# Summing softmax denominators four tiles at a time on VectorE, with a new planning figure for the exponential

## Chip, cores, metric

The kernel runs on one core of one Trainium2 chip. The metric is the device time of one execution in microseconds (us), and the time of a version is the median of its runs.

## What is computed

A pre-normalised transformer layer in bf16 on 2,048 tokens of width 1,024, with 32 heads of 32 columns and a hidden width of 3,584:

```python
h  = x + attention(layernorm(x), wqkv, wo)      # softmax(q k^T / sqrt(32)) v, 32 heads
h2 = h + gelu(layernorm(h) @ w1 + b1) @ w2 + b2
```

Every score is exponentiated once: 2,048 x 2,048 x 32 numbers. Besides the product with V, each row of exponentials must be summed, since that sum is the softmax's denominator.

## The kernel before

**Tiles.** Heads are handled in eight groups of four (g) and queries in eight blocks of 256 (qb), so there are 64 jobs. A job runs eight rounds; a round covers 256 keys. The score product of a round, `qk`, is eight row-tiled matmuls (line 805) into four PSUM banks. ScalarE exponentiates them with two instructions of 128 x 1024 (line 816) into one of nine buffers `PT` (a few early rounds use other buffers, which the profile calls `PX`). The product with V, `pv`, is eight column-tiled matmuls (line 842) which accumulate in one half of a PSUM bank.

**Denominators.** VectorE first adds the two key tiles of a round (line 857, 128 x 1024 bf16 into a ring of three buffers `PS`). TensorE then adds that pair sum over the partitions with four column-tiled matmuls against a tile of ones (`den`, line 871), accumulating in the other half of the job's bank. Round 7 of a job (and every odd round of the first three jobs, the lead) skips VectorE and gives its exponentials to eight `den` matmuls directly. A job so makes seven pair sums, and its `den` of one round is put behind the `pv` of the next. The pair sum has the highest priority on VectorE (-2); draining a projection or an FFN bank has 0, the pieces of the gelu have 1.

**Background.** Everything else on TensorE (projections, output product `wo`, `ffn1`, `ffn2`) is "background". It fills the time between score products. It uses PSUM banks 6 and 7, of which the running job holds one. In the attention the kernel goes through query blocks in order; `wo(u)`, the second layer norm, `ffn1(u)`, the gelu (five VectorE instructions of 128 x 1024 and one tanh on ScalarE per four tiles, lines 1020 to 1025) and `ffn2(u)` of block u run beneath the attention of later blocks. After the last exponential there remain `wo(7)`, layer norm, `ffn1(7)`, half of `ffn2(6)` and `ffn2(7)`.

**What sets the order.** A list scheduler in the kernel's Python simulates all engines with a cost per instruction and writes out one fixed instruction order per engine, with semaphore waits. `c_act` is the planned duration of a ScalarE instruction: for 1,024 columns 0.064 + 1024/1200 = 0.917 us. `c_dve(1024, 2)` plans 0.598 us for a pair sum; a `pv` is planned at 0.22 us, a `den` of one pair sum at 0.11, a change of TensorE's tiling at 0.104. A ready `qk` always goes first on TensorE; background goes in between until the next `qk` is ready in the plan; ready `pv` and `den` wait in a group. Where no background is ready in two stretches of the plan (`KEEP`), dummy matmuls of line 1203 fill in.

The order holds on the chip whatever the real durations are: an engine that gets to an instruction early waits for its semaphore, and one that is late holds up what stands behind it.

Of the kernel before, what the change touches and what calls it, by code (L numbers as in the profile page):

```python
# [8 lines left out]
ALU = mybir.AluOpType  # L9
# [328 lines left out]
def build_kernel(nc, A_x, A_wqkv, A_wo, B_w1, B_b1, B_w2, B_b2, out):  # L338
# [22 lines left out]
    class Area:  # L361
# [3 lines left out]
        def take(self, shape, dtype, align=64):  # L365
            n = mybir.dt.size(dtype)
            for d_ in shape[1:]:
                n *= d_
            self.cur = -(-self.cur // align) * align
            off = self.cur  # L370
            self.cur += n
            assert self.cur <= TOP, (shape, self.cur - TOP)
            return off, n

    def sb(area, name, shape, dtype, split=1, parts=1):


        off, n = area.take(shape, dtype)
        h = nc.alloc_sbuf_tensor_at(name, shape, dtype, offset=off)
        step = n // split  # L380
        bufs = []
        for i in range(split):
            ps = [gr.buf("SB", off + i * step, off + (i + 1) * step, (name, i)) for _ in range(parts)]
            bufs.append(ps if parts > 1 else ps[0])
        return h, (bufs if split > 1 else bufs[0])
# [31 lines left out]
    PS, B_PS = sb(top, "PS", [P, NS, 4, 256], BF, NS)  # L417
# [107 lines left out]
    def c_dve(n, x=1):  # L525
        return (62 + n / x) / 960.0

    def c_act(n, ap_bias=False):
        return (0.064 if n == 1024 else 0.073) + (0.093 if ap_bias else 0.0) + n / 1200.0

    def pe(fns, occ, reads=(), writes=(), kind="bg", mode="full", prio=0, after=()):
        return gr.add(E.PE, fns, occ, 0.225 if isinstance(fns, list) and len(fns) > 1 else 0.2, reads, writes, prio, kind, mode, after)
# [7 lines left out]
    def bi(bank):  # L540
        return bank.n if isinstance(bank, Slot) else bank
# [33 lines left out]
    def act(fn, n, reads=(), writes=(), prio=0, ap_bias=False, kind="", after=()):  # L575
        return gr.add(E.Activation, fn, c_act(n, ap_bias), 0.16, reads, writes, prio, kind, after=after)

    def dve(fn, occ, reads=(), writes=(), prio=0, after=()):
        return gr.add(E.DVE, fn, occ, 0.135, reads, writes, prio, after=after)
# [13 lines left out]
    def dma_transpose(out_ap, in_ap, nbytes, reads, writes, prio):  # L593
# [5 lines left out]
         reads=[B_ident], writes=[B_ident])  # L599
# [222 lines left out]
    PV_START = 6  # L822

    closing = set()

    class Job:

# [7 lines left out]
        def pv(self, r, s):  # L835
            g, bank, first = self.g, self.bank, self.n == 0
            last = self.n == 7
            self.n += 1
            fns = []
            for i in range(2):  # L840
                for h in range(4):
                    fns.append(lambda p, i=i, h=h: p.matmul(  # L842
                        psum[32 * h:32 * h + 32, bi(bank), 0:256], V[:, g, 2 * r + i, 32 * h:32 * h + 32],
                        PTs[s][:, h // 2, h % 2, 256 * i:256 * i + 256], start=first and i == 0, stop=last and i == 1,
                        tile_position=(0, 32 * h), skip_group_check=True))
            rd = B_PTs[s] + [B_V[NT * g + 2 * r], B_V[NT * g + 2 * r + 1]]
            t = pe(fns, 0.22, reads=rd, writes=[self.B_O, self.B_D] if first else [self.B_O], kind="pv", mode="col")
            take(t, bank)
            while self.sums:
                self.den(*self.sums.pop(0), False)  # L850
            if r == 7 or self.g == 0 and self.qb < NLJ and r % 2:
                self.sums.append((s, True))
            else:
                n = cnt["ps"] % NS
                cnt["ps"] += 1
                pairs = PTs[s][:, :, :, :].rearrange("p u j c -> p (u j) c")
                dve(lambda v: v.tensor_tensor(PS[:, n, :, :], pairs[:, :, 0:256], pairs[:, :, 256:512], ALU.add), c_dve(1024, 2),  # L857
                    reads=B_PTs[s], writes=[B_PS[n]], prio=-2, after=hold if self.g == 0 and self.qb < NLJ else ())
                self.sums.append((n, False))
            if last:  # L860
                while self.sums:
                    self.den(*self.sums.pop(0), not self.sums)
                self.finish()
# [199 lines left out]
    for k in range(80):  # L1063
        pe(lambda p: p.matmul(psum[:, 6, 0:256], ident[:, :], b2t[:, 0:256], start=True, stop=True), 0.18 if k < 42 else 0.115,
           reads=[B_ident, B_b2t], writes=[B_ps[6]], kind="warm")
    LEAD_ACT = (0, 1, 2, 3)
    LEAD_PE = 10
    NLJ = 3
# [21 lines left out]
    for hc in range(8):  # L1090
# [7 lines left out]
        for k, r in [(k, hc) for k in range(min(hc, NLJ))] + ([(hc, r) for r in range(hc + 1)] if hc < NLJ else []):  # L1098
            n = 8 * k + r
# [199 lines left out]
def bass_sequential_preLN__softmax_full_mha__dense_activation_gelu__prompt_kernel(  # L1299
    nc: bass.Bass,  # L1300
    A_x: bass.AP,
    A_wqkv: bass.AP,
    A_wo: bass.AP,
    B_x: bass.AP,
    B_w1: bass.AP,
    B_b1: bass.AP,
    B_w2: bass.AP,
    B_b2: bass.AP,
    out: bass.AP,
):  # L1310
    build_kernel(nc, A_x, A_wqkv, A_wo, B_w1, B_b1, B_w2, B_b2, out)
# [28 lines left out]
```

## Time and profile before

| what | before |
|---|---|
| median of 3 runs | 1080.26 us (1077.96 to 1081.25) |
| the profiled execution | 1079.06 us; span in the profile 1077.3 us |
| TensorE busy (modelled ends) | 1053.3 us, 98% |
| ScalarE busy | 1013.3 us, 94% |
| VectorE busy | 747.3 us, 69% |
| granted TensorE clock | 1.0 |
| exponentials | 1,024 of 128 x 1024, from 15.0 us to 1010.8 us |
| pair sums on VectorE (line 857) | 439, 686 ns median duration |

Times in the profile are microseconds from the start of the span. The recorded duration of an instruction includes a part that overlaps its neighbour on the same engine, so durations of a full engine add up to more than its busy time; how often an engine can take such an instruction has to be read from successive starts or successive ends. The chain of waits is followed from the last instruction back to what released it.

### The profile page before, as it was taken

What the parts mean: (1) busy time and instruction counts of PE and PEld (TensorE: products, weight loads), DVE (VectorE), ACT (ScalarE), POOL (GpSimd) and SP (SyncE); (2) the same over time, 40 slices, a digit from 0 to 9 for tenths busy, and PEclk for the clock granted to TensorE, in tenths of its full rate; (3) what the DMA queues carried; (4) which work ended last, traced back from release to release, by engine and by line L of the source; (5) the groups of instructions that cost most, each with busy time, mean ns of one, the idle gap of its engine ahead of it and who ended that gap; (6) DMA issues with size and microseconds to landing.
All of it is one profiled execution on the core that took longest, in us unless ns stands there. A gap on an engine that the chain in (4) does not pass through costs nothing.

```text
span 1077.3 us, 41835 instructions
## 1 busy us (share of the span) xinstructions
PE 1053.3 (98%) x19071; PEld 609.4 (57%) x19071; DVE 747.3 (69%) x1438; ACT 1013.3 (94%) x1116; POOL 45.4 (4%) x110
## 2 busy tenths in 40 slices
PE   8999999999999999999999999999999999999998
PEld 6576555554444754674475457447545754575483
DVE  8776666566576895698489659948975976696401
ACT  4999999999999999999999999999999999999650
POOL 4200000000010000001000100100010000000100
PEclk9999999999999999999999999999999999999999
DMA  8561543438473555655664764466375555866260
GB/s 223 166 172 30 159 134 119 138 119 297 165 186 130 188 191 181 232 181 169 217 240 164 209 230 179 154 223 230 144 232 205 186 200 181 294 220 250 94 244 19
DMA packets 136177, 196.37 MB, mean 182 GB/s; under 512 B 49216, under 2 KB 100288, under 8 KB 133184
## 3 DMA queue, kind: packets, MB, share of 16 engines
q1 hardware_dynamic: 136000, 193.70, 54.0%
q8 instruction: 149, 2.44, 0.9%
q14 instruction: 28, 0.23, 0.1%
HBM read 177.94 MB, written 27.26 MB: 190 GB/s over the span
## 4 chain that ended last, share of the span: by engine, by line
ACT 60%; PE 33%; DVE 4%; POOL 1%; issue 1%; DMA 0%; SPq 0%; POOLq 0%; DVEq 0%
ACT PT L816 55%; PE ps L568 11%; PE ps L565 7%; PE ps L571 5%; PE ps L805 5%; PE ps L842 3%; ACT PX L816 3%; ACT uu L1023 2%; PE ps L871 2%; DVE PS L857 1%; DVE st L617 1%; DMA xrb<-in_A_x_dram 0%; DVE gT L1001 0%; DVE gT L1025 0%; POOL denb L626 0%
## 5 line engine op out<-in xcount | busy, mean ns | idle before, releaser
L816 ACT ACTIVATE PT<-ps 128x1024 bf16<-128x1024 f32 x992 | 922.0, 1094 | 5.9 <-PE ps L805 5.7
L857 DVE TENSOR_TENSOR PS<-PT 128x1024 bf16<-128x1024 bf16 x431 | 285.3, 685 | 132.4 <-PE ps L871 67.6
L805 PE MATMUL ps<-QT,KT 32*128 32x256 bf16 x4096 | 203.9, 273 | 5.6 <-ACT PT L816 2.7
L842 PE MATMUL ps<-PT,V 128*32 128x256 bf16 x3968 | 174.2, 273 | 2.1 <-ACT PT L816 1.7
L805 PEld LDWEIGHTS ps<-QT,KT 32*128 32x128 bf16 x4096 | 61.0, 92 | 161.4 <-ACT PT L816 135.9
L871 PE MATMUL ps<-PS,ones 128*32 128x256 bf16 x1756 | 122.0, 274 | 2.3 <-DVE PS L857 1.2
L842 PEld LDWEIGHTS ps<-PT,V 128*32 128x32 bf16 x3968 | 101.7, 97 | 28.5 <-issue 7.0
L568 PE MATMUL ps<-hnT,a_w1r 128*128 128x256 bf16 x940 | 114.5, 273 | 0.6 <-DVE gT L1001 0.5
L565 PE MATMUL ps<-a_w2r,gT 128*32 128x512 bf16 x1436 | 102.2, 381 | 0.1
L568 PEld LDWEIGHTS ps<-hnT,a_w1r 128*128 128x128 bf16 x940 | 86.8, 98 | 24.4 <-issue 13.7
L568 PE MATMUL ps<-a_w2r,gT 128*128 128x512 bf16 x397 | 97.6, 381 | 0.8 <-DVE hch L966 0.6
L565 PE MATMUL ps<-hnT,a_w1r 128*32 128x256 bf16 x2512 | 89.8, 274 | 3.5 <-DVE OD L894 1.5
L1001 DVE TENSOR_TENSOR gT<-ps,b1f 128x512 bf16<-128x512 f32 x98 | 67.3, 686 | 16.0 <-PE ps L568 8.0
L565 PEld LDWEIGHTS ps<-hnT,a_w1r 128*32 128x32 bf16 x2512 | 61.8, 96 | 19.5 <-issue 16.5
L1046 DVE SCALAR_TENSOR_TENSOR hch<-ps,hch 128x512 bf16<-128x512 f32 x32 | 21.9, 685 | 70.5 <-PE ps L571 47.1
L871 PEld LDWEIGHTS ps<-PS,ones 128*32 128x32 bf16 x1756 | 46.2, 96 | 26.6 <-DVE PS L857 8.6
L568 PEld LDWEIGHTS ps<-a_w2r,gT 128*128 128x128 bf16 x397 | 33.7, 98 | 46.5 <-issue 13.0
L568 PE MATMUL ps<-xnT,Wall 128*128 128x512 bf16 (+1 forms) x272 | 57.4, 346 | 0.4 <-ACT xnT L645 0.2
L1023 ACT ACTIVATE uu<-uu 128x1024 bf16<-128x1024 bf16 x49 | 54.3, 1113 | 0.0
L565 PEld LDWEIGHTS ps<-a_w2r,gT 128*32 128x32 bf16 x1436 | 32.0, 96 | 25.4 <-issue 13.5
L622 POOL CAST mvb<-mv 128x2 bf16<-128x2 f32 (+1 forms) x25 | 5.2, 216 | 972.5 <-DVE mv L619 972.5
L568 PE MATMUL ps<-wov,OT 128*128 128x512 bf16 x146 | 35.4, 380 | 1.4 <-DVE OD L894 0.8
(93 smaller groups left out, 1020.8 us busy)
## 6 DMA issues: line engine op xcount, KB each, us to landing
a_w2r<-w_blocks SPq DMA_DIRECT2D x105, 512.0 KB, 5.2
a_w1r<-w_blocks SPq DMA_DIRECT2D x98, 512.0 KB, 3.5
wov<-wo_blocks SPq DMA_DIRECT2D x16, 1024.0 KB, 4.8
w_blocks<-in_B_w_dram SPq DMA_DIRECT2D x28, 512.0 KB, 3.9
b_w1r<-w_blocks SPq DMA_DIRECT2D x14, 512.0 KB, 3.9
a_w1r<-in_A_wqkv_dram SPq DMA_DIRECT2D x11, 512.0 KB, 5.5
Wall<-in_A_wqkv_dram SPq DMA_DIRECT2D x17, 256.0 KB, 4.9
xrb<-in_A_x_dram SPq DMA_DIRECT2D x16, 256.0 KB, 4.7
```

Of the source, the lines that this page charges most:

```text
L565: fns.append(lambda p, j=j: p.matmul(psum[32 * j:32 * j + 32, bi(bank), c0:c1], lhsT[:, 32 * j:32 * j + 32], rhs, start=start, stop=stop, ...
L568: t.whole = lambda p: p.matmul(psum[:, bi(bank), c0:c1], lhsT, rhs, start=start, stop=stop, skip_group_check=True)
L571: t = pe(lambda p: p.matmul(psum[:, bi(bank), c0:c1], lhsT, rhs, start=start, stop=stop), occ, reads=reads, writes=[bb(bank)], mode="full" ...
L617: dve(lambda v, c=c, k=k, x_ap=x_ap: v.bn_stats(st_l[:, i + k, 6 * c:6 * c + 6], x_ap[:, 512 * c:512 * c + 512]), 0.595, reads=B_x if isin ...
L805: return p.matmul(psum[:, 2 * us[h // 2] + h % 2, 256 * i:256 * i + 256], KT[32 * h:32 * h + 32, g, k0:k0 + P], QT[32 * h:32 * h + 32, qs, :],
L816: act(lambda a, u=u, k=k: a.activation(PTs[s][:, k, :, :], psum[:, 2 * u:2 * u + 2, :], ACT.Exp, bias=0.0, scale=SCALE), 1024, reads=[B_ps ...
L842: fns.append(lambda p, i=i, h=h: p.matmul(psum[32 * h:32 * h + 32, bi(bank), 0:256], V[:, g, 2 * r + i, 32 * h:32 * h + 32], PTs[s][:, h / ...
L857: dve(lambda v: v.tensor_tensor(PS[:, n, :, :], pairs[:, :, 0:256], pairs[:, :, 256:512], ALU.add), c_dve(1024, 2), reads=B_PTs[s], writes ...
L871: fns.append(lambda p, h=h, rhs=rhs, i=i: p.matmul(psum[32 * h:32 * h + 32, bi(bank), 256:512], ones32[:, :], rhs, start=False, stop=last, ...
L1001: t = dve(lambda v: v.tensor_tensor(g[:, fc:fc + 2, :], psum[:, bi(bank), :].rearrange("p (f c) -> p f c", f=2), b1f[:, fc:fc + 2].unsquee ...
L1023: act(lambda a: a.activation(w, w, ACT.Tanh, bias=0.0, scale=KT2), 1024, reads=[B_uu[i]], writes=[B_uu[i]], prio=-1)
L1046: drop(dve(lambda v, hs=hs, bank=bank, half=half: v.scalar_tensor_tensor(hch[:, hs, c], psum[:, bi(bank), :], half, hch[:, hs, c], ALU.mul ...
```

## The change

Two edits. In every job but the three of the lead, the pair sums of rounds 0 and 1 are added on VectorE into one sum of four tiles, and so are those of rounds 2 and 3; TensorE then gets one `den` for each. Rounds 4, 5, 6 and 7 stay as they were. The sum of four is written in place into the ring buffer of the odd round, with the same priority as a pair sum. And the planner's figure for a ScalarE instruction of 1,024 columns becomes 0.051 + 1024/1200 = 0.904 us; besides the exponentials the 49 tanh instructions and the six copies of 1,024 columns use it.

```diff
     def c_act(n, ap_bias=False):
-        return (0.064 if n == 1024 else 0.073) + (0.093 if ap_bias else 0.0) + n / 1200.0
+        return (.051 if n == 1024 else 0.073) + (0.093 if ap_bias else 0.0) + n / 1200.0
...
     closing = set()
+    FOURS = (0, 2)
...
-                self.sums.append((n, False))
+                four = not (self.g == 0 and self.qb < NLJ)
+                if four and r in FOURS:
+                    self.half = n
+                elif four and r - 1 in FOURS:
+                    o = self.half
+                    dve(lambda v: v.tensor_tensor(PS[:, n, :, :], PS[:, n, :, :], PS[:, o, :, :], ALU.add), c_dve(1024, 2),
+                        reads=[B_PS[n], B_PS[o]], writes=[B_PS[n]], prio=-2)
+                    self.sums.append((n, False))
+                else:
+                    self.sums.append((n, False))
```

The whole order is planned anew, so the order of instructions may differ anywhere.

## The prediction

> **What bounds the kernel now.** I read the page first, then the chain of waits in order of time, then the ScalarE timeline, then TensorE's timeline around the `den` matmuls, then the busy times of the stretches with gelu.
>
> ```profile
> span 1077.3 us, 41835 instructions
> ...
> PE 1053.3 (98%) x19071; PEld 609.4 (57%) x19071; DVE 747.3 (69%) x1438; ACT 1013.3 (94%) x1116; POOL 45.4 (4%) x110
> ...
> ACT 60%; PE 33%; DVE 4%; POOL 1%; issue 1%; DMA 0%; SPq 0%; POOLq 0%; DVEq 0%
> ...
> L816 ACT ACTIVATE PT<-ps 128x1024 bf16<-128x1024 f32 x992 | 922.0, 1094 | 5.9 <-PE ps L805 5.7
> L857 DVE TENSOR_TENSOR PS<-PT 128x1024 bf16<-128x1024 bf16 x431 | 285.3, 685 | 132.4 <-PE ps L871 67.6
> ```
>
> ScalarE is idle before exponentials of `PT` for only 5.9 us. The chain in order of time says when it is the limit:
>
> ```profile
> 64.09 251.43 ACT PT L816 x274
> ...
> 978.62 30.36 ACT PT L816 x33
> ...
> 1025.57 48.81 PE ps L571 x336
> ```
>
> For 251 us the chain is nothing but exponentials, at 251.43/274 = 0.918 us each. Up to 1010.8 us the kernel is paced by ScalarE, with TensorE close behind; the last 66.5 us are TensorE's FFN work behind the last exponential. A saving counts only if it shortens one of those two.
>
> The change says that an exponential takes 0.904. ScalarE's timeline, each row two neighbouring exponentials (start, duration from the first's start to the second's end):
>
> ```profile
> 261.28 1.99 ACT L816 ACTIVATE PT<-ps 128x1024 bf16<-128x1024 f32 x2
> ...
> 262.18 2.00 ACT L816 ACTIVATE PT<-ps 128x1024 bf16<-128x1024 f32 x2
> ...
> 263.09 2.01 ACT L816 ACTIVATE PT<-ps 128x1024 bf16<-128x1024 f32 x2
> ...
> 269.42 2.10 ACT L816 ACTIVATE PT<-ps 128x1024 bf16<-128x1024 f32 x2
> ...
> 270.32 2.11 ACT L816 ACTIVATE PT<-ps 128x1024 bf16<-128x1024 f32 x2
> ...
> 271.38 1.97 ACT L816 ACTIVATE PT<-ps 128x1024 bf16<-128x1024 f32 x2
> ```
>
> Starts follow each other by 0.90 us, so that is where 0.904 comes from. But each row is 0.01 longer than the one before: the ends (start plus duration) are 263.27, 264.18, 265.10, then 271.52, 272.43, 273.35, that is 0.91 to 0.92 apart. The lead of the starts grows until one start is held back by 1.06 (270.32 to 271.38), and the ends don't notice. Taken over all exponentials, end to end is 0.917 in the median and never under 0.912. What dependents wait for is the end. So ScalarE's rate is 0.917, which is what the old figure planned, and it is already full: summing, over ScalarE's neighbours from 27 us to 1010.8, what each end-to-end step has above 0.917 (exponential) or 0.937 (tanh) gives only **6.1 us lost**. The largest pieces are 0.93 us at 924, 0.73 at 425, 0.55 at 756, 0.37 at 738, 0.30 at 808, 0.29 at 907 and 0.27 at 362. That is all that the attention can gain.
>
> **The change part by part.**
>
> *The `den` matmuls removed.* 61 jobs lose two each: 122 groups of four.
>
> ```profile
> 992.15 0.29 PE L871 MATMUL ps<-PS,ones 128*32 128x256 bf16 x4
> 992.27 0.39 PE L842 MATMUL ps<-PT,V 128*32 128x256 bf16 x8
> 992.49 0.28 PE L871 MATMUL ps<-PS,ones 128*32 128x256 bf16 x4
> 992.60 0.39 PE L842 MATMUL ps<-PT,V 128*32 128x256 bf16 x8
> ```
>
> From start to start, `pv` takes 0.22 us and `den` 0.11. So 122 x 0.11 = **13.4 us of TensorE** come free, 0.11 x 2/8 = 27 ns a round. None is on the path as such, since ScalarE paces these rounds.
>
> *The new figure.* The plan believes a round takes 2 x 0.904 = 1.808 us and not 1.834, and gives TensorE 26 ns less between two score products. With the 27 ns freed, background per round stays as it was, within 1 ns. The two edits cancel for the background and add up for slack: on the chip the round still lasts 1.834, so TensorE reaches each `qk` earlier relative to ScalarE, and waits there. Now it comes late: from the end of the exponential that frees the last bank to the first `qk` matmul it is 0.25 us in the median over 510 rounds, where the promptest take 0.055. ScalarE bears this, because one more exponential is then still running, but a hitch of 0.3 us more starves it. With 26 ns gained per round the 0.2 us are made good in some eight rounds. I expect most stalls that come from small slips to go. Two of them, at 425 and 924, go with a TensorE gap of 0.5 to 0.7 us marked "issue", which the change doesn't remove; earlier arrival takes about 0.2 off each, which leaves 0.5 + 0.7. I leave 0.8 for all others. Gain: 6.1 - 2.0 = **4.1 us**; bounds 6.1 (no stall left) and 0 (VectorE makes as many new ones), or below nothing as in the first rival.
>
> *VectorE's added work.* 122 adds. Independent neighbours of this shape start 0.60 us apart; an instruction that needs the result of the one before it starts 0.716 after it (975.16 to 975.88, lines 1020 to 1021). The sum of four needs the pair sum just written, so 0.60 to 0.72 each, 73 to 88 us; I take 0.66, 80 us, because another instruction often stands in between. VectorE goes to about 827 us, 77%, which is nothing on average but not everywhere. [...]
>
> ```profile
> 940.50:979.80 39.30, 38.30 (x847) 26.67 (x849) 37.36 (x71) 39.30 (x44) 0.00 (x0) 1.00 0.62 220
> ```
>
> In this row (columns: length, PE, PEld, DVE, ACT, POOL) of the last gelu stretch, VectorE has 1.9 us idle in 39.3. It gets 39.3/1.834/4 = 5.4 more adds, 3.5 us, so this gelu ends some 2 us later, and likewise the six before. Gelu pieces have the lowest priority, so bank drains still pass them; what waits is `ffn2`, whose last weights need the last gelu.
>
> *What covers that.* In the last cycle background runs dry twice: from 921.6 to 932.6 us (11 us with dummy matmuls, while block 6's layer norm is on its way) and from 1002.7 to 1009.4 (6.7 us, when `ffn2(6)` is through and `wo(7)` waits for the last job). Six gelus at 2 us make 12 us of lag before the first gap, which takes 11; the seventh's 2 us and the 1 left over fit in the second. So the tail starts as before, and I cost VectorE's part at nothing. Its price without that cover is in the rival.
>
> *The ring.* Today VectorE stands for 68.2 us before pair sums whose ring buffer TensorE hasn't read; TensorE stands little for VectorE:
>
> ```profile
> DVE PS L857 <- PE ps L871: 68.2, 60, 5.6
> ...
> PEld ps L871 <- DVE PS L857: 8.6, 29, 0.7
> ```
>
> After the change the even round's buffer comes free when VectorE has added it, so two of seven returns no longer wait for TensorE. Behind a `den` that waits for a late sum of four stand `pv`, background and the next `qk`, and ScalarE waits for that; the plan issues a `den` only once its sum is done in the plan, and real time is 1.4% longer than the plan's, so I cost it at nothing between -1 and +3 us.
>
> *Lead and tail.* The lead makes no sums of four, and the last job's chain from the last exponential to `wo(7)` has none near its end: 0.
>
> **Sum.** 1079.06 (span 1077.3 and 1.76 around it) - 4.1 = 1074.96 for an execution like the profiled one. The median of the runs is 1.2 above that one, so **1076.2** for a median: 0.38% faster.
>
> **The rivals.**
> - *Slower: VectorE becomes the limit of the gelu stretches.* For: those stretches are 95 to 97% full, and every sum goes ahead of the gelu. If each stretch loses the full 5.4 x 0.72 = 3.9 us of background, the first six lose 23, the first gap takes 11, and of 12 + 3.9 the second takes 6.7: 9 us move into the tail, 1089 with no gain elsewhere; half that loss with some new ScalarE stalls makes 1084 to 1086. It decides from (11 + 6.7)/7 = 2.5 us per stretch. Against: a late gelu can be passed by other background. Chance 0.31.
> - *No change: stalls are replaced.* Sums of four that come late hold `den`, and the new ones eat the 4 us; 1077 to 1083.5, about 1080. Chance 0.25.
> - *The exponential really takes 0.904.* Then the old plan held ScalarE back by 13 ns x 1,024 = 13 us, and TensorE's 13.4 us let it go: 1067. Against: ends 0.917 apart also from 262 to 265 us, where dummy matmuls show that TensorE had time. Chance 0.04. [...]
>
> **How the numbers follow.** A measurement of this kernel can tell about 0.3%, 3.2 us, from no change. Forecast 0.40 (its own range 1073.5 to 1077.0; the floor is 1080.26 - 6.1 = 1074.2, less some scatter of the runs), which with the last rival makes faster 0.44; same 0.25; slower 0.31. The range goes from 1072, which leaves out the last rival, to 1087, which leaves out the upper part of the first.
>
> **What would show it.** Line 871 with 488 fewer matmuls on `PS`; line 857 still 439, with 122 more adds on VectorE; VectorE busy near 827. Exponentials still 0.917 from end to end. `qk` nearer to the exponential that frees it. ScalarE's loss after 27 us at about 2 us; last exponential near 1006.7; from there still 66.5 us. I am wrong if the ends come 0.904 apart, if background matmuls of `ffn2(6)` run behind the last exponential that didn't before, or if ScalarE loses 6 us or more.

## The result and the profile after

The changed kernel takes 1082.86 us in the median of 11 runs against 1080.81 for the kernel before: a ratio of 1.0022, with a 95% interval of 1.0011 to 1.0032. The forecast was 0.38% faster; it is 0.22% slower, 2.1 us. The profiled execution is 4.0 us longer than that of before (spans 1081.3 and 1077.3).

The page of the changed kernel:

```profile
span 1081.3 us, 40425 instructions
...
PE 1032.5 (95%) x18254; PEld 594.5 (55%) x18322; DVE 822.3 (76%) x1560; ACT 1011.7 (94%) x1116; POOL 50.6 (5%) x110
...
ACT 74%; PE 18%; DVE 4%; issue 1%; POOL 1%; DMA 1%; SPq 0%; POOLq 0%; DVEq 0%
...
L816 ACT ACTIVATE PT<-ps 128x1024 bf16<-128x1024 f32 x992 | 922.4, 1171 | 10.5 <-PE ps L805 10.4
L858 DVE TENSOR_TENSOR PS<-PT 128x1024 bf16<-128x1024 bf16 x431 | 293.1, 687 | 115.5 <-ACT PT L816 83.6
```

TensorE has 21 us less work, VectorE 75 us more, and ScalarE's share of the chain has risen from 60% to 74%: the changed kernel hangs on ScalarE more than before, as wanted. Yet ScalarE stands 10.5 us for score products and not 5.9. The sums of four are line 865, 122 of them, 83.5 us of recorded time.

Where the 4.0 us are: the first exponential ends at 17.0 us and not 16.0 (the rows before it wait 4.6 us for the DMA of `x` and not 3.7; single profiles of the kernels below differ here by up to 1.2 us). From 27 us on, ScalarE loses **9.1 us** against 6.1, measured end to end as in the prediction. Behind the last exponential there are 66.55 us against 66.46. So 1.0 + 3.0 + 0.1, within rounding.

Those 9.1 us are of another kind. I sort ScalarE's losses by size: pieces under 0.25 us sum to 2.6 us before and **0.6 after**; pieces of 0.25 us or more sum to 3.4 before and **8.5 after**, in ten places. Six of the ten, 5.5 us together, look like this one (TensorE's and VectorE's timeline; start, duration, instruction, and the idle time ahead of it):

```profile
839.42 0.28 PE L881 MATMUL ps<-PS,ones 128*32 128x256 bf16 x2
839.59 0.69 DVE L858 TENSOR_TENSOR PS<-PT 128x1024 bf16<-128x1024 bf16 x1
841.42 0.29 PE L881 MATMUL ps<-PS,ones 128*32 128x256 bf16 x2 [1.72 <-issue]
```

Line 881 is the `den` group of four. Two of its matmuls run at 839.42, and the other two come 2.0 us later. No semaphore can stand there, since the kernel's waits come ahead of a group and never inside it. The profile says "issue": it shows nothing that TensorE waited for. The DMA section of the page shows what the program itself costs, of the kernel before and of the changed one:

```profile
q8 instruction: 149, 2.44, 0.9%
```

```profile
q8 instruction: 144, 2.36, 0.9%
```

149 packets of 16 KB for the 38,142 recorded TensorE instructions of before is one packet for 256 instructions, from which I take q8 for the queue of TensorE's program. The packets start from 16.3 to 1,047.6 us there, so the program arrives while it runs, and a packet takes 0.96 us in the median. The gap above ends 1.44 us after the end of a packet; the six gaps that cost ScalarE time end 1.31 to 1.53 us after one.

The place of the gaps in the program says the same more sharply. Counted in recorded TensorE instructions from the start (two for each weight load and its matmul, one for each semaphore instruction), all six gaps stand behind instruction 193 or 194 of a run of 256. So do 65 of the 109 gaps of 0.5 us or more between two weight loads of the same line and tile that the 18 profiles of this document have from 20 to 1,065 us; no other of the 256 places has more than two. With one packet for 256 instructions I take this place for the one where one packet's instructions end and the next one's begin, a packet end, and call a gap there a program gap.

The six come behind dense stretches: in the 4 us ahead of each, TensorE had issued 128 to 135 weight loads, with a matmul each some 256 to 270 instructions, where the median 4 us hold 71 and the 95th percentile is 127. The packet whose end the gap's end follows began only 0.3 to 1.7 us before TensorE stopped; why it began no earlier, no run shows. Narrow matmuls (four of 32 columns in place of one of 128) make such stretches, because they need four times the instructions for the same work: 112 to 127 of the weight loads ahead of each gap are of 32 columns.

### The profile page after: what moved, and what is told of

Read it like the earlier page. It is cut to its first block, busy times and chain, and to the rows that moved or that the text cites. A ratio compares the mean times of both kernels' runs of the same rounds, so it can differ in the third digit from the quotient of the medians.

```text
span 1081.3 us, 40425 instructions
## 1 busy us (share of the span) xinstructions
PE 1032.5 (95%) x18254; PEld 594.5 (55%) x18322; DVE 822.3 (76%) x1560; ACT 1011.7 (94%) x1116; POOL 50.6 (5%) x110
## 4 chain that ended last, share of the span: by engine, by line
ACT 74%; PE 18%; DVE 4%; issue 1%; POOL 1%; DMA 1%; SPq 0%; POOLq 0%; DVEq 0%
ACT PT L816 68%; PE ps L571 5%; PE ps L568 5%; ACT uu L1033 3%; PE ps L565 3%; ACT PX L816 3%; PE ps L805 2%; PE ps L843 1%; DVE PS L858 1%; DVE st L617 1%; PE ps L881 1%; DMA xrb<-in_A_x_dram 1%; POOL denb L626 0%; DMA q_scratch<-lq 0%; POOL rden L628 0%
## 5 line engine op out<-in xcount | busy, mean ns | idle before, releaser
L816 ACT ACTIVATE PT<-ps 128x1024 bf16<-128x1024 f32 x992 | 922.4, 1171 | 10.5 <-PE ps L805 10.4
L858 DVE TENSOR_TENSOR PS<-PT 128x1024 bf16<-128x1024 bf16 x431 | 293.1, 687 | 115.5 <-ACT PT L816 83.6
L843 PE MATMUL ps<-PT,V 128*32 128x256 bf16 x3968 | 164.7, 273 | 2.3 <-issue 1.2
L568 PE MATMUL ps<-a_w2r,gT 128*128 128x512 bf16 x431 | 106.5, 380 | 6.4 <-issue 2.1
L881 PE MATMUL ps<-PS,ones 128*32 128x256 bf16 x1268 | 87.9, 274 | 4.1 <-issue 1.7
L565 PE MATMUL ps<-a_w2r,gT 128*32 128x512 bf16 x1208 | 88.0, 381 | 2.3 <-DVE OD L904 1.3
L865 DVE TENSOR_TENSOR PS<-PS 128x1024 bf16<-128x1024 bf16 x122 | 83.5, 685 | 2.0
L568 PEld LDWEIGHTS ps<-a_w2r,gT 128*128 128x128 bf16 x454 | 38.8, 98 | 55.9 <-issue 14.1
L568 PE MATMUL ps<-xnT,Wall 128*128 128x512 bf16 (+1 forms) x288 | 61.7, 348 | 2.2 <-issue 1.1
L881 PEld LDWEIGHTS ps<-PS,ones 128*32 128x32 bf16 x1268 | 33.4, 96 | 20.0 <-issue 6.9
L568 PE MATMUL ps<-wov,OT 128*128 128x512 bf16 x163 | 40.9, 380 | 2.7 <-issue 1.3
```

Source lines behind the costliest of these rows:

```text
L565: fns.append(lambda p, j=j: p.matmul(psum[32 * j:32 * j + 32, bi(bank), c0:c1], lhsT[:, 32 * j:32 * j + 32], rhs, start=start, stop=stop, ...
L568: t.whole = lambda p: p.matmul(psum[:, bi(bank), c0:c1], lhsT, rhs, start=start, stop=stop, skip_group_check=True)
L816: act(lambda a, u=u, k=k: a.activation(PTs[s][:, k, :, :], psum[:, 2 * u:2 * u + 2, :], ACT.Exp, bias=0.0, scale=SCALE), 1024, reads=[B_ps ...
L843: fns.append(lambda p, i=i, h=h: p.matmul(psum[32 * h:32 * h + 32, bi(bank), 0:256], V[:, g, 2 * r + i, 32 * h:32 * h + 32], PTs[s][:, h / ...
L865: dve(lambda v: v.tensor_tensor(PS[:, n, :, :], PS[:, n, :, :], PS[:, o, :, :], ALU.add), c_dve(1024, 2), reads=[B_PS[n], B_PS[o]], writes ...
L881: fns.append(lambda p, h=h, rhs=rhs, i=i: p.matmul(psum[32 * h:32 * h + 32, bi(bank), 256:512], ones32[:, :], rhs, start=False, stop=last, ...
```

## The experiments

Two theories were set against each other. P: the new plan is as good as forecast, but has more and longer program gaps. V: VectorE's added sums hold up TensorE. Times are ratios of medians to the kernel before on the same chip, each with its 95% interval.

**The two parts alone.**

```diff
-        return (.051 if n == 1024 else 0.073) + ...      # fours_only
+        return (0.064 if n == 1024 else 0.073) + ...
```
```diff
-        return (0.064 if n == 1024 else 0.073) + ...     # figure_only, in the kernel before
+        return (.051 if n == 1024 else 0.073) + ...
```

> The sums of four with the old figure of 0.917. Theory P (the new plan's TensorE stands without a program more often: gaps in the middle of a group of matmuls that end 1.3 to 1.5 us after the last packet of an instruction fetch; ScalarE lost 5.6 us behind such gaps after the change and 2.0 before): the adds themselves cost little, TensorE reaches the score products as late as before (0.2 to 0.3 us in the median), ScalarE loses 4 to 8 us after 27 us depending on how many program gaps fall on it, time 1079 to 1083. Theory V (VectorE's 122 adds hold up bank drains, and these the score products): no slack from the figure, so as slow as the change or slower, 1083 or more, with most of ScalarE's loss behind gaps that wait for VectorE.

> The figure of 0.904 without the sums of four. P: score products come promptly (0.15 us or less in the median) and the many small losses of 0.03 to 0.3 us are gone, program gaps stay; background has 26 ns a round less, 13 us in all, of which the two gaps in the last cycle (11 and 6.7 us) take most, so the tail grows by 0 to 3 us; time 1078 to 1083. V: without the adds nothing new holds TensorE up, faster than before by 3 to 4 us, 1077.

The sums of four alone: 0.9994 (0.9982 to 1.0005). The first `qk` matmul comes 0.23 us after the exponential that frees its bank, as before (0.25; in the changed kernel 0.11), and the small pieces of loss stay at 2.1 us. ScalarE lost 9.3 us in the profile, where 4 to 8 were forecast. So the adds show no cost by themselves. Whether they bring anything this ratio can't tell, as the moved programs and the granted clock below show.

The figure alone: 1.0066 (1.0049 to 1.0083), slower than either theory expected. The small pieces do go (0.1 to 0.3 us are left, by the size from which a loss is counted). But background that no longer fits between score products comes behind the last exponential, 70.5 us in place of 66.5, and the new plan has a hole of its own, in this ScalarE row:

```profile
731.36 3.77 ACT L816 ACTIVATE PT<-ps 128x1024 bf16<-128x1024 f32 x4 [6.10 <-PE ps L842]
```

ScalarE stands 6.1 us for a `pv` to free an exponential buffer, while TensorE runs background first. So the figure brings the promptness, and with the sums of four as well neither the longer tail nor this hole is there. The hole belongs to this one order; the ratio of 1.0066 is not the price of the figure in general.

**Moving the program, not the plan.** 32 or 64 of the dummy matmuls at the start are split in two halves after planning, which leaves the order and its waits as they were and moves every later TensorE instruction by 64 or 128, a quarter or half of a packet (for 192, 48 are split in two and 16 in four).

```diff
     gr.merge_tiles()
+    for t in [t for t in gr.tasks if t.kind == "warm"][:64]:
+        t.fns = [lambda p, h=h: p.matmul(psum[:, 6, 128*h:128*h+128], ident[:, :], b2t[:, 128*h:128*h+128], start=True, stop=True) for h in range(2)]
```

> The changed kernel with 64 of the dummy matmuls at the start split in two, so that all later TensorE instructions lie 128 further in the program (half a fetch of 16 KB); plan and order are the same. P: the program gaps fall on other places, ScalarE's loss behind them changes from 5.6 us to anything between 2 and 8, and the time by as much; the losses at 94 and 314 us, which follow waits for VectorE and a DMA, stay where they are unless a gap precedes them. V: the same losses at the same times, 1082 to 1083.

> The changed kernel, unaltered, to see how far the places of the program gaps repeat. P: the same order and the same program lie at the same places, so at least half of the six gaps that cost ScalarE time (361, 584, 647, 741, 841 and 981 us) are there again within 5 us; median 1082 to 1084. Rival R (gaps come at random from run to run and the shifted kernel was lucky): other places, and a median nearer to 1080.

> The changed kernel with 32 dummy matmuls split in two: all later TensorE instructions 64 further in the program. P: again other places for the gaps, a median of its own between 1077 and 1084, repeatable within its runs. R: 1080 as the others.

> The kernel before with its TensorE program moved by 128 instructions. P: alignment matters here as well; a median that differs from 1080.4 by 1 to 3 us in either direction, with ScalarE's small losses of 0.03 to 0.3 us (some 4 us together) unchanged. R: no difference.

> The kernel before with its TensorE program moved by 64 instructions. P: as with 128, a median of its own, within 3 us of 1080.4; the mean of the three alignments of before tells with the three of the changed kernel what the change is worth apart from alignment: I expect the changed kernel lower by 0 to 2 us. R: no difference.

> The changed kernel, TensorE's program moved by 192 instructions, the fourth quarter of a fetch. Medians of the other three against before: 1.0022, 0.9980 and 0.9983. P: between 0.998 and 1.003; with it the mean over the quarters says what the change is worth apart from alignment.

> The kernel before, moved by 192 instructions. The other three against before: 1, 1.0014 and 0.9991. P: 0.999 to 1.002, so that the mean of the changed kernel lies 0.5 to 2 us lower than that of before.

| moved by | before: ratio | small, large pieces, us | changed: ratio | small, large pieces, us |
|---|---|---|---|---|
| 0 | 1 | 2.6, 3.4 | 1.0022 (1.0011 to 1.0032) | 0.6, 8.5 |
| 64 | 1.0014 (1.0002 to 1.0027) | 3.6, 6.8 | 0.9980 (0.9967 to 0.9992) | 0.3, 6.1 |
| 128 | 0.9991 (0.9978 to 1.0004) | 2.5, 4.1 | 0.9983 (0.9972 to 0.9994) | 0.7, 6.8 |
| 192 | 1.0026 (1.0014 to 1.0039) | 3.3, 6.4 | 1.0001 (0.9989 to 1.0012) | 0.7, 7.8 |
| mean | 1.0008 | 3.0, 5.2 | 0.9997 | 0.6, 7.3 |

The same plan, the same work and a few split dummies: the changed kernel spreads over 0.42%, 4.5 us, and that of before over 0.35%. The result of 1.0022 is the changed kernel's worst quarter against a good one of before. Run again unmoved, the changed kernel gave 1.0015 (1.0003 to 1.0028), and all six gaps were there again within 2 us, each behind the same weight load, counted from the start of the program. Their lengths vary: ScalarE lost 11.6 us in this profile, 10.9 of it in large pieces. This is the one from above in the second profile:

```profile
838.83 0.28 PE L881 MATMUL ps<-PS,ones 128*32 128x256 bf16 x2
841.42 0.28 PE L881 MATMUL ps<-PS,ones 128*32 128x256 bf16 x2 [2.31 <-issue]
```

Moved by 64, the changed kernel has gaps behind weight loads 11,306, 14,743 and 17,415 of its program, as it had unmoved (at 647, 841 and 982 us), though other matmuls now stand there. So the gaps belong to the program's layout, not to chance; rival R falls, and V can't explain the spread, as VectorE's work is the same in all four. In the mean over the quarters the changed kernel is 0.11%, 1.2 us, faster than before, but single quarters differ by up to 0.42%, so four a side don't settle the sign.

Nor does the changed plan lose more to program gaps, as P had it. The large pieces that start within 4 us of a gap at a packet's end sum to 3.2, 6.5, 3.6 and 5.2 us in the four alignments of before (mean 4.6) and to 5.5, 3.8, 3.8 and 3.7 in those of the changed kernel (mean 4.2). The two profiles first compared have the least and the second most of these eight. The forecasts of the medians held, but for before moved by 192 (0.999 to 1.002 forecast, 1.0026 measured); before moved by 128 lies at the edge of its range (1.0 us of 1 to 3). The before side's expectation of unchanged small losses held (2.5 to 3.6 us). That the changed kernel would keep its losses where a wait for VectorE or a DMA makes them held for the one at 95 us, not for the one at 314 us.

**The granted clock.** A second thing moves these times. In seven of the 18 profiles the granted TensorE clock falls to half well inside the span, for 3.41 us (6.83 us in that of the sums of four alone). The repeat of the changed kernel and its first profile in the same 3.41 us, and before moved by 64 behind its last exponential (length; busy time and number of instructions of PE, PEld (TensorE's weight loads), DVE, ACT, POOL; granted clock; DMA share, GB/s):

```profile
842.83:846.24 3.41, 3.41 (x25) 1.93 (x21) 2.76 (x5) 1.94 (x2) 0.00 (x0) 0.50 0.06 17
```

```profile
842.83:846.24 3.41, 3.41 (x44) 2.52 (x41) 3.34 (x7) 3.28 (x4) 0.00 (x0) 1.00 0.34 111
```

```profile
1013.33:1016.74 3.41, 3.41 (x18) 0.71 (x18) 0.59 (x1) 1.70 (x2) 0.00 (x0) 0.50 0.50 154
```

TensorE starts 25 matmuls where it started 44. ScalarE loses 1.6 us at the end of this drop, a piece that the first profile doesn't have; 1.4 and 1.8 us of the changed kernel's large pieces moved by 128 and 192 stand at such drops too. In before moved by 64 and by 128 the drop falls behind the last exponential, and from there to the end it takes 68.0 and 68.1 us in place of 66.5. In the timed runs of before on one chip the medians are 1079.4 us for ten executions with a mean clock of 1.0, 1080.4 for eleven with 0.998 and 1081.6 for eight with 0.997; on another they are 1079.9, 1081.8 and 1084.1. One drop lowers the mean clock by 0.0016, so a drop costs one to two us.

Drops are not spread evenly: 43 of 116 executions of before have none, 42 of 58 of the changed kernel in its four alignments, all 6 with the figure alone, none of the 12 with the sums of four alone. What sets one off, no run here shows. Taking only executions without one, 3 to 13 of a kernel, the four alignments are at 1, 1.0008, 0.9992 and 1.0029 for before and at 1.0018 (the repeat), 0.9987, 0.9990 and 1.0013 for the changed kernel. So the spread between alignments stays, and of the 1.2 us of the means some 0.6 remain.

**Fewer instructions.** The kernel makes a stretch of narrow background matmuls whole if it lasts 3.0 us. A lower threshold does the same work with fewer instructions and more changes of tiling. In the trace of before a `pv` takes 0.22 us up to a `den` of its own tiling (1003.70 to 1003.92) and 0.32 up to a whole matmul (1011.32 to 1011.64), so a change took 0.10 us there; the expectations below take 0.12.

```diff
-            if k == 0 or sum(x.occ for x in run[k:]) >= 3.0:
+            if k == 0 or sum(x.occ for x in run[k:]) >= 1.0:     # 0.5 in the merge05 kernels
```

> The changed kernel where a stretch of narrow background matmuls is made into whole matmuls from 1.0 us on instead of 3.0 us (same work, a quarter of the instructions, one change of tiling of about 0.12 us more each). P: TensorE's program gets shorter, program gaps that cost ScalarE time fall from six to two or fewer, ScalarE loses 2 to 5 us instead of 9, time 1077 to 1080. V: VectorE's work is the same, 1082 to 1084, or slower by the changes of tiling.

> The changed kernel with whole matmuls from 1.0 us on, its TensorE program moved by 64 instructions. P (program gaps make the spread between alignments): with fewer instructions less hangs on alignment, so within 1.5 us of the 1079.3 that this threshold gave unmoved, where the changed kernel itself spreads over 4 us; pieces of ScalarE's loss over 0.25 us sum to 3 to 6. R (the threshold's gain was one more lucky alignment): anything from 1077 to 1084.

> As the run before it, moved by 128 instructions. P: 1077.5 to 1081. R: 1077 to 1084.

> The kernel before with whole matmuls from 1.0 us on. P: the plan leaves TensorE no slack there (score products 0.25 us late), so each further change of tiling, about 0.12 us, costs ScalarE time as often as a program gap saved gives it back: 1079 to 1083, no better than before by more than 1 us. Rival: the threshold is a gain by itself, 1077 to 1078.

> The changed kernel with whole matmuls from 0.5 us on. P: still fewer instructions and program gaps, but a change of tiling of 0.12 us in most rounds, against 26 ns of slack a round and what TensorE waits for ScalarE: the small losses come back; 1078 to 1082.

> The changed kernel with whole matmuls from 0.5 us on, moved by 128 instructions. P: with 1,581 weight loads fewer than the changed kernel little hangs on alignment: within 1 us of the 1078.0 it gave unmoved. R: 1077 to 1082.

| kernel | weight loads | ratio |
|---|---|---|
| changed | 18,322 | 1.0022 (1.0011 to 1.0032) |
| changed, 1.0 us | 17,923 | 0.9987 (0.9977 to 0.9998) |
| changed, 1.0 us, moved by 64 | 17,955 | 0.9971 (0.9958 to 0.9983) |
| changed, 1.0 us, moved by 128 | 17,987 | 0.9993 (0.9980 to 1.0006) |
| changed, 0.5 us | 16,741 | 0.9971 (0.9957 to 0.9985) |
| changed, 0.5 us, moved by 128 | 16,805 | 0.9954 (0.9939 to 0.9969) |
| before, 1.0 us | 18,579 | 1.0059 (1.0039 to 1.0080) |

At 1.0 us the spread over three quarters is 0.22%, where the changed kernel has 0.42% over the same three; medians 1079.3, 1077.8 and 1080.5. Moved by 64 it lies 1.5 us from the unmoved one in medians and 1.7 by ratios, at the edge of its forecast. The forecast of two gaps or fewer in the unmoved one was missed: three remained that cost time, and ScalarE lost 6.2 us where 2 to 5 were forecast. Against the changed kernel at the same alignment it is faster unmoved and by 64, and slower by 128 (0.9993 against 0.9983), so a gain of the 1.0 us threshold isn't shown.

At 0.5 us the medians are 1078.0 and 1077.3, at both alignments faster than the changed kernel. In the first profile two program gaps cost ScalarE 0.8 and 0.2 us, in the second one costs 0.4 at most. The small pieces come back as forecast, some 2 us. The change with 0.5 us, moved by 128, is the best version run and beats both kernels: 0.46% faster than before. None of its executions has a clock drop; against those of before without one (7 of 23) it is 0.26% faster. Its page:

```profile
span 1074.8 us, 37363 instructions
...
q8 instruction: 132, 2.16, 0.9%
...
ACT 77%; PE 17%; DVE 3%; DMA 1%; POOL 1%; issue 1%; SPq 0%; POOLq 0%; DVEq 0%
```

Twelve packets fewer, and ScalarE on 77% of the chain. ScalarE loses 3.6 us there. The 1.0 us threshold makes the kernel *before* 0.59% slower, at 1087.5 us, outside its forecast of 1079 to 1083: small pieces rise to 4.0 us and large ones to 8.6. Nearly all of the large ones (8.3 us) start within 4 us of a program gap, and five of its six executions have a clock drop. So fewer weight loads don't by themselves mean less loss to program gaps. That the slack of the change is what pays for the changes of tiling is a likely reading, but with one alignment of before it isn't shown.

**The loss at 95 us.** All five profiles of the changed kernel have a piece of about 1.4 us there (1.38 to 1.54), and so have all of it with merged matmuls. The figure alone has 0.27 there, before none, and the sums of four alone have 0.95, but of another form: 52 background matmuls ahead of a score product. VectorE's rows in the changed kernel:

```profile
92.91 0.69 DVE L858 TENSOR_TENSOR PS<-PT 128x1024 bf16<-128x1024 bf16 x1 [1.07 <-PE ps L881]
93.52 0.69 DVE L742 CAST V<-ps 128x512 bf16<-128x512 f32 x1
```

A pair sum waits for TensorE to read its ring buffer, the bank drain of the V projection stands behind it, and TensorE then waits for the drain:

```profile
94.26 0.29 PE L565 MATMUL ps<-Wall,xnT 128*32 128x256 bf16 x4 [0.31 <-DVE V L742]
```

```diff
-                four = not (self.g == 0 and self.qb < NLJ)
+                four = self.g > 1 or self.qb >= NLJ           # with 0.5 us as above
```

> As the changed kernel with whole matmuls from 0.5 us on, but without sums of four in the three jobs of head group 1. At 96 us every profile of the changed plan has a loss of 1.38 us, at whatever alignment, where 2.9 us lie between two score products while the bank drain on VectorE stands behind a pair sum that waits for TensorE. If the sums of four in group 1 make it, it goes, and the time falls to about 1076.6; if the new figure or the order makes it, it stays or moves: 1078.

The piece shrinks from 1.38 to 0.38 us, so the sums in the first three jobs of head group 1 (or the order that comes with them) make 1.0 us of it. The time is 1078.0, ratio 0.9962 (0.9947 to 0.9977), within the other merged versions: a program gap at 998 us and one at 644 us cost 1.3 and 0.9 us and took what was saved. The forecast of 1076.6 was missed.

## Why the prediction was wrong

*ScalarE's rate and floor: right.* Told that an exponential takes 0.904, the chip goes on ending one every 0.917 us (median end to end in both profiles, with starts 0.904 apart in both). The rival with 0.904 is out.

*Freed TensorE time and the cancelling: right.* 488 fewer `den` matmuls on `PS` (1,268 against 1,756). The figure alone pushed 4 us of background into the tail; with the sums of four the tail is unchanged.

*Promptness: right in kind and near in size.* Median 0.25 to 0.11 us, a gain of 0.14 where 0.2 was expected; 233 of 510 score products now start within 0.1 us of the exponential that frees them, 69 before:

```profile
PEld ps L805 <- ACT PT L816: 156.9, 454, 1.7
```

(135.9 us and 398 times before.) Small pieces fell from 3.0 to 0.6 us in the mean of four alignments.

*VectorE: right.* Busy 822.3 us against 827 forecast, and a sum of four starts 0.726 us after its pair sum in the median, near the 0.716 taken for dependent neighbours. The lag came much as costed: block 6's `ffn1` starts at 937.6 us in place of 932.6, with other background in the whole of the first gap. Of these 5 us, 3.0 are ScalarE's, since the exponential of the same number starts that much later; 2 are left over, where 1 was forecast, and the second gap hides them. The rival that puts this lag in the tail did not happen. The ring got looser, 25.8 us in place of 68.2:

```profile
DVE PS L858 <- PE ps L881: 25.8, 44, 1.6
```

*The step that failed* is one term of the gain: "Two of them, at 425 and 924, go with a TensorE gap of 0.5 to 0.7 us marked 'issue', which the change doesn't remove", left at 0.5 + 0.7, with 0.8 for all others: 2.0 us in all. Measured were 9.1: 5.5 behind six program gaps where 1.2 were counted, and 3.6 elsewhere where 0.8 were counted. I took the program gaps of one profile for a constant of the kernel. As the moved programs show, they depend on where packets of 256 instructions end in one plan, and a new plan draws them again: the loss behind them is 3.2 to 6.5 us over four alignments of before and 3.7 to 5.5 over those of the changed kernel. That the profile of before had the least of the first four and the changed kernel's the most of the second was luck of the draw. Arriving early didn't cover the gaps: the six, with 0.4 to 1.7 us of idle time, cost 0.55 to 1.7 us.

The other miss is smaller and not luck: 1.4 us at 95 us, at every alignment, a ring wait with a drain behind it and TensorE behind that. The prediction's paragraph on the ring came near this form and costed it at nothing, between -1 and +3 us.

With the means over the four alignments the account closes. On small pieces 2.4 us are gained. On large pieces 2.1 are lost: 1.4 at 95 us and 0.8 at clock drops, some 0.3 at other waits, less 0.4 that program gaps cost fewer. Behind the last exponential 0.7 are gained, all of it from the two clock drops of before, and 0.1 is lost ahead of the first. That makes 0.9 us; the mean spans of the profiles differ by 1.0, and the medians by 1.2. So what the plan itself shows in the mean is a gain of 2.4 and a loss of 1.4 us, 1 us where 4.1 were forecast. These are single profiles: the repeat of the changed kernel differed by 2.5 us in ScalarE's loss. Left open are what sets off a clock drop, and why 236 of 288 packet ends behind at least 126 weight loads in 4 us have no gap of 0.5 us.

## What to carry to other kernels

Before a difference of a few tenths of a per cent between two instruction orders is explained, move the program of the busiest engine by a part of a packet without changing the order: what that moves (up to 0.42% here) is not the edit's. Compare the granted clock of the executions as well, since a drop cost one to two us here. In this order, written out beforehand, ScalarE paces the rest and gained nothing from an optimistic planning figure (0.917 us an exponential under both); but TensorE then reached it earlier (0.11 us behind the exponential that frees a bank, not 0.25), and this removed small stalls (3.0 to 0.6 us), with the sums of four paying for the work displaced; without them 4 us of it came behind the last exponential. Look for "issue" ahead of an instruction in the middle of a group, as the 1.72 us ahead of 841.42. Narrow tilings buy fewer changes of tiling with four times the instructions; whole matmuls from 0.5 us on were the cheaper choice in the changed kernel (0.9971 and 0.9954), from 1.0 us on in the kernel before they were not (1.0059).

## What the runs showed of the hardware that I had not expected

Queue q8 moved 149 packets of 16 KB in the profile of before, one for 256 recorded TensorE instructions, and 144 in that of the changed kernel, from the first 20 us on to the stretch behind the last exponential and 0.96 us each in the median. At some packet ends TensorE stood, often in the middle of a group of matmuls: over the 18 profiles 84 of them have a gap of 0.5 to 2.6 us, which ends 1.2 to 1.9 us (1.4 in the median) after the next packet's end. 52 of the 84 stand behind at least 126 weight loads in 4 us. 64 instructions more at the start of the program changed the median of the same order by 0.38% on one chip (1082.7 to 1078.6 us). That a gap is TensorE's wait for its next packet is my reading of these numbers; no row of a profile says it.

In seven of the 18 profiles the granted TensorE clock fell to 0.50 well inside the span, for 3.41 us in six and 6.83 in one. By a mean clock under 1.0 there was a drop in 73 of 116 executions of before and in 16 of 58 of the changed kernel; in the medians a drop cost one to two us.
